# A recurrent attention block with a gated layer behind it: a triangular inverse in 33 instead of 37 schedule items, and a chunk's preparation one chunk later

## Chip, core and metric

The kernel runs on one core of a Trainium2 chip. A core has five engines with a queue of instructions each: the tensor engine (PE in the profile; PEld is its loading of weights), the vector engine (DVE), the scalar engine (ACT), GpSimd (POOL) and the sync engine (SP), which here issues nearly all DMA transfers. The metric is the device time of the whole kernel in microseconds, the median of several runs.

## What is computed

The first block is a recurrence over 768 time steps for 4 batches of 8 heads of width 40; its output is the input of a gated layer with 3072 tokens, width 320 and 2048 hidden units:

```python
for t in range(S):
    kt, vt, rt = (k[:, :, t], v[:, :, t], r[:, :, t])
    wt, at, bt = (w[:, :, t], a[:, :, t], b[:, :, t])
    y[:, :, t] = np.einsum('bhd,bhde->bhe', rt, state)
    Sa = np.einsum('bhde,bhe->bhd', state, at)
    state_decay = state * wt[:, :, None, :] - np.einsum('bhd,bhe->bhde', Sa, bt)
    state = state_decay + np.einsum('bhd,bhe->bhde', vt, kt)
...
h = x @ w_in
g = h * np.cos(h)
out = g @ w_out
```

## The kernel before, in words

Time is cut into 24 chunks of 32 steps. Within a chunk the recurrence is solved in closed form, for which a 32 by 32 lower triangular system per batch and head has to be inverted; from chunk to chunk only the state is handed on. The program issues every instruction in an order that is written out by hand: a list of segments for each chunk c (`segs`, lines 1056 to 1093), each segment a small function. The engines run their own queues in that order, so the list decides what stands ahead of what on each engine.

The segments are these.

- **Main work of chunk c** (`main`, line 954), which must follow the previous chunk: `t` (transposes of the state, tile sT), `q` (tile qps), `x` (tile x0ps, copied out by ACT at line 625 and DVE at line 626), `s` (tile sps: the inverse, `G["rt", c]`, times that copy, line 629), `z` (tile dps: the new state, DVE lines 682 and 689, POOL lines 683 and 694). Two steps after z the output y is written to DRAM and read back transposed as xT (`tokens`, line 699).
- **Preparation of the next chunk** (`p2`, line 946): `v`, `k`, `g` with tiles vT, kT, gram; g ends with DVE lines 567 and 573, which free the PSUM tile gram. All these PSUM tiles come from one pool of two buffers, `at` (line 325), so each one waits for the release of the last but one.
- **Preparation of two chunks at a time, well ahead** (`p1`, line 917): `pw` (W: eight transposes wT, ACT copies, POOL lines 381 and 392, and the reciprocal of W at line 396 with the product bn on POOL at line 397), `pa` (a~: eight transposes aps, DVE line 402 twice, and the reciprocal of the pair's second chunk), `pb` (b~: transposes bT) and `pn` (N: the matrices to invert, tile nps). pa also puts the loads of the next pair's w, a and b on SP, two and more steps later (lines 931 to 935).
- **The inverse of a group of four chunks** (`inverse`, line 507), all on DVE but for a POOL memset: a start (transpose, line 478), 31 steps with j from 31 down to 1 (a product, line 488, and a subtraction, line 492, over j(32 - j) elements per partition), an end (transpose, line 501). `s` of the group's first chunk can't be issued before the end has been.
- **Pieces of the gated layer**, each M in a list standing for one: A (`first_a`, tile ph, with three DVE sums of an earlier piece at lines 810 to 812), B (`first_b`, the rest of ph, then ACT line 759, DVE line 761, ACT lines 765 and 766, DVE line 769, where `turns` is h minus its rounding), and two S pieces (`second`/`products`, tile po). A of chunk pair g needs xT of that pair.

The function `step` (line 347) issues one segment or piece, then what has become due of the delayed work (`later`: loads, stores, copies), and then takes items of the pending inverse: one item a step from chunk 5 on. So an inverse is spread over some forty steps, one item behind each. Items may be empty; four of the 37 are, right behind the start. When a list comes to `s` and the inverse has not ended, lines 1105 to 1109 first issue one more piece with up to four items behind it.

The inverse of chunks 8 to 11 begins behind pn in chunk 6 and ends in chunk 8, that of 12 to 15 begins in chunk 10, and so on for 16 and 20. In the lists of before, W and a~ of chunks 12 and 13 are prepared in chunk 7 (those of 16 and 17 in 11, of 20 and 21 in 15), b~ and N of the same chunks in chunk 8 (12, 16); W and a~ of chunks 14 and 15 in chunk 9, b~ and N in chunk 10, behind which the next inverse begins. `scanned` (line 939) multiplies up the decays of a later group on DVE (lines 171 and 176, 4.0 us together) in chunks 4, 8 and 12.

Of the kernel before, what the change touches and what calls it, by code (L numbers as in the profile page):

```python
# [20 lines left out]
def kernel(  # L21
# [45 lines left out]
    P, C, DP = 128, 32, 64  # L67
# [53 lines left out]
    for n, fill in (("w", 1.0), ("a", 0.0), ("b", 0.0)):  # L121
        for i in range(4):
            x = slice((i - 2) * H * DP, (i - 1) * H * DP)
            if i < 2:
                t = const.tile([P, H, DP], F32, tag=f"nat_{n}{i}", name=f"nat_{n}{i}")
            else:
                t = {
                    "w": w_in_sb[:, 0, late:], "a": w_in_sb[:, 1, late:], "b": late_out
                }[n][:, x].rearrange("p (h d) -> p h d", h=H)
# [4 lines left out]
    for n in "kvr":  # L134
        t = const.tile([P, H, D], F32, tag=f"nat_{n}", name=f"nat_{n}")
# [370 lines left out]

    def inverse(c):
        return [
            lambda: inv_start(c), *[lambda: None] * (4 if c >= 8 else 0),
            *(lambda j=j: inv_step(j) for j in range(C - 1, 0, -1)), lambda: inv_end(c)  # L510
        ]


# [448 lines left out]
    with tc.manual_schedule():  # L962

        w_work = weights()
        w_count = [0]

        def counted(work):
            work()
            w_count[0] += 1

        w_steps.extend([w_work[0][1], w_work[1][1], w_work[0][2]])
        for n, (*_, product) in enumerate(w_work):
            nxt = n + 5 if n < 5 else n + 3 if n >= 7 else len(w_work)
            w_steps.append(lambda f=product: counted(f))
            if nxt < len(w_work):
                w_steps.append(w_work[nxt][0])
            if n + 1 < len(w_work):
                w_steps.append(w_work[n + 1][2])
            if n + 2 < len(w_work):
                w_steps.append(w_work[n + 2][1])  # L980

        def all_of(steps, n=None):
            for work in steps[:n]:
                work()
            del steps[:n]

        def busy(n, after=False):


            ps = ps_h.tile([P, 512], F32, tag="h", name="busy")  # L990
            if after:
                nc.vector.memset(tick, 1.0)
                nc.tensor.matmul(
                    ps[:1, :], lhsT=tick, rhs=pick(idle, 0, (0, 4), (1, P)), start=True, stop=True, skip_group_check=True
                )
            for _ in range(n):
                mm(ps, idle, pick(idle, 0, (0, 4), (1, P)), True)

        def shifted(n):


            ps = at("pad")
            for _ in range(n):
                mm(ps[:1, 0, :1], idle[:, :1], idle[:, :1], True)


        G["w1"] = sb2.tile([P, 2, 4 * B, C], F32, tag="gT", name="w1")
        nc.vector.memset(G["w1"], 0.0)
        first, other = p1(0), p1(2)
        for seg in (*first[:2], *other[:2], *first[2:], *other[2:]):  # L1010
            step(seg)
        scanned(1)
        p2_in(0)
        p2_kn(0)
        inv_steps.extend(inverse(0))
        v, k, g = p2(0)
        v1, k1, g1 = p2(1)
        for n, seg in ((12, v), (0, k), (0, g), (6, main(0)[2]), (6, None), (4, v1), (0, k1), (0, g1)):
            for _ in range(n):
                inv_steps.pop(0)()  # L1020
            if seg:
                step(seg)
            else:
                for m in range(3):
                    w_work[m][0]()
                p2_in(1)
                p2_kn(1)
        N_PAD = {0: 111, 19: 75}
        shifted(N_PAD[0])
        while inv_steps:  # L1030
            inv_steps.pop(0)()
            if 2 < len(inv_steps) < 9:
                busy(1, True)
        for m in range(3, 5):
            w_work[m][0]()

        done = 0

        def piece(*fill):
            nonlocal done  # L1040
            _, work, j, need = pieces[done]
            while w_steps and w_count[0] < need[j]:
                w_steps.pop(0)()
            step(work, *fill)
            done += 1

        def allowed(c):
            return done < len(pieces) and 2 * pieces[done][0] + 2 <= c

        M = object()  # L1050
        for c in range(NCH):
            t, q, x, s, z = main(c)
            v, k, g = p2(c + 1) if c + 1 < NCH else [lambda: None] * 3
            q0 = c - c % 4 + 4
            fill, pn, pn4 = (1, 4), None, None
            if c == 0:
                segs = [s, z]
            elif c == 1:
                segs = [t, v, q, k, x, g, s, z]
            elif c == 2:  # L1060
                segs, fill = [t, v, q, k, M, x, M, g, M, s, M, z, M, M], (0, 2)
            elif c == 3:
                pw4, pa4, pb4, pn4 = p1(4)
                pw, pa, pb, pn = p1(6)
                segs = [
                    t, pw4, M, q, pa4, M, x, lambda: scanned(2), M, s, pw, M, pb4, pa, M, pn4, M, z, M,
                    pb, v, pn, k, M, g,
                ]
                fill = (2, 3)
            elif c == 4:  # L1070
                pw, pa, *p8 = p1(8)
                segs = [t, v, M, q, M, k, x, M, M, M, M, pw, s, M, z, M, g, M, pa, lambda: scanned(3)]
                fill = (2, 0)
            elif c == 5:
                pw, pa = p1(10)[:2]
                pb, pn = p8
                segs = [t, M, pb, q, M, pn, k, M, x, M, s, pw, v, M, z, M, g, M, pa, M]
            elif c % 4 == 0 and q0 < NCH:
                pb, pn = p1(q0)[2:]
                segs = [t, v, M, q, M, k, x, M, g, M, s, pb, M, z, M, pn, M, M]  # L1080
                if q0 + 4 < NCH:
                    segs.insert(-1, lambda: scanned(c // 4 + 2))
            elif c % 4 == 1 and q0 < NCH:
                pw, pa = p1(q0 + 2)[:2]
                segs = [t, M, pw, q, M, x, k, M, s, v, M, z, M, pa, M, g, M, M]
            elif c % 4 == 2 and q0 < NCH:
                pb, pn = p1(q0 + 2)[2:]
                segs = [t, M, pb, q, M, pn, v, M, x, M, s, k, M, g, M, z, M, M]
            elif c % 4 == 3 and q0 + 4 < NCH:
                pw, pa = p1(q0 + 4)[:2]  # L1090
                segs = [t, M, pw, q, M, x, k, M, s, v, M, z, M, pa, M, g, M, M]
            else:
                segs = [t, v, M, q, M, x, k, M, g, M, s, M, M, z, M, M]
            n = len(segs)

            goal = 8 * (c + 1) - (18 if c < 19 else 20)
            empty, places = 0, segs.count(M)
            if c > 3:
                empty = max(0, min(places - (goal - done), 2 if c < 8 else places))
                goal = max(goal, done + places - empty)  # L1100
            place = 0
            if c == 19:
                shifted(N_PAD[c])
            for i, seg in enumerate(segs):
                while seg is s and ("rt", c) not in G:
                    if allowed(c):
                        piece(4, 0)
                    else:
                        inv_steps.pop(0)()
                while seg is pn4 and w_steps:  # L1110
                    w_steps.pop(0)()
                if seg is not M:
                    step(seg, *fill, small=seg in (q, x, g, s, z, pn, pn4))
                    if c < 2 or c == 2 and not done:
                        busy({s: 6, q: 5, v: 4, k: 4, z: 4}.get(seg, 3))
                else:
                    place += 1
                    if place * empty // places > (place - 1) * empty // places:
                        continue
                    if allowed(c) and (c != 4 or done < 23):  # L1120
                        piece(*fill)
                while i == n - 1 and c > 3 and done < goal and c != 4 and allowed(c):
                    piece(*fill)
                if seg is pn and (c == 3 or c > 4 and c % 4 == 2):
                    inv_steps.extend(inverse(q0))
        for g, work, j, _ in pieces[done:]:
            if g == NCH // 2 - 1 and j == 0:
                while waiting:
                    step(lambda: None)
            step(work)  # L1130
        while waiting:
            step(lambda: None)
# [29 lines left out]
```

## Time and profile before

| | before |
|---|---|
| time, median of 3 runs (lowest to highest) | 854.71 us (853.95 to 854.74) |
| span of the profiled execution | 849.2 us |
| PE busy in it | 738.0 us (87%) |
| DVE busy | 582.4 us (69%) |
| ACT busy | 378.7 us (45%) |
| POOL busy | 248.6 us (29%) |
| mean clock granted to PE | 0.937 |
| one reciprocal, DVE line 396 | 2.14 us |
| start and end of an inverse, DVE lines 478 and 501 | 1.24 and 1.93 us |

The page of the profile gives each engine's busy time, and below it the span in 40 equal slices, each digit the busy share in tenths. A line of a wait list reads "engine, tile and line that waited <- engine, tile and line that released it: us in total, times, longest". A line of a timeline begins with the start in us from the beginning of the span and the duration in us; "out<-in" are the program's names for the tiles, followed by shapes and, in brackets, the idle time of the engine just before and what ended it.

### The profile page before, as it was taken

How to read it: one execution, taken by the hardware profiler on the slowest of the kernel's cores; microseconds unless marked ns; L12 is line 12 of the kernel's file. 1: busy time of each engine (PE TensorE's matmuls, PEld its weight loads, DVE VectorE, ACT ScalarE, POOL GpSimd, SP SyncE). 2: the span in 40 equal slices, each digit the busy share in tenths (PEclk: the TensorE clock that was granted, in tenths of full speed). 3: DMA queues.
4: the chain of work that ended last, by engine and by line, in shares of the span. 5: the costliest groups of instructions: out<-in, count | busy, mean ns of one | idle time of the engine just before them, and what ended most of it. 6: DMA issues, size and time to landing. Idle time of an engine off the chain costs nothing.

```text
span 849.2 us, 38915 instructions
## 1 busy us (share of the span) xinstructions
PE 738.0 (87%) x17312; PEld 614.7 (72%) x17312; DVE 582.4 (69%) x1266; ACT 378.7 (45%) x697; POOL 248.6 (29%) x420
## 2 busy tenths in 40 slices
PE   3557778896899988999978999889999897999996
PEld 2434456674577877888867888768888787888875
DVE  6988878778734788675897664997466865444444
ACT  1216686454254425345435444534653442453442
POOL 5305544220524531231430331331233132122100
PEclk9758789998989989999998999999999998999999
DMA  7367562353243314234223323223220220201000
GB/s 122 82 128 217 132 159 77 55 123 55 55 100 66 69 24 76 52 95 70 54 40 61 71 55 67 50 47 59 46 44 25 39 43 21 40 20 35 20 16 15
DMA packets 183302, 55.74 MB, mean 66 GB/s; under 512 B 157152, under 2 KB 178656, under 8 KB 183136
## 3 DMA queue, kind: packets, MB, share of 16 engines
q1 hardware_dynamic: 180560, 51.95, 28.8%
q8 instruction: 136, 2.23, 1.1%
q10 hardware_dynamic: 2320, 0.98, 0.6%
q0 software_dynamic: 256, 0.33, 0.2%
q14 instruction: 30, 0.25, 0.1%
HBM read 42.07 MB, written 11.14 MB: 63 GB/s over the span
## 4 chain that ended last, share of the span: by engine, by line
PE 55%; DVE 20%; ACT 8%; DMA 5%; SPq 5%; issue 5%; POOL 3%; POOLq 0%; DVEq 0%; ACTq 0%
PE ph L102 21%; PE po L102 14%; SPq L153 5%; PE dps L102 4%; DVE inv_tmp L488 3%; PE x0ps L102 2%; PE vT L331 2%; DVE rw L396 2%; DVE turns L761 2%; ACT turns L766 2%; PE sps L102 2%; PE gram L102 2%; PE nps L102 2%; ACT turns L765 2%; DVE inv L492 1%
## 5 line engine op out<-in xcount | busy, mean ns | idle before, releaser
L102 PE MATMUL ph<-xT,w_in_sb 128*128 128x256 f32 x768 | 193.5, 398 | 5.4 <-DVE gT L769 4.6
L102 PEld LDWEIGHTS ph<-xT,w_in_sb 128*128 128x128 f32 x768 | 144.2, 197 | 35.5 <-issue 14.6
L759 ACT ACTIVATE turns<-ph,rnd 128x512 f32<-128x512 f32 x96 | 64.0, 686 | 173.9 <-PE ph L102 173.5
L761 DVE SCALAR_TENSOR_TENSOR turns<-turns,ph 128x512 f32<-128x512 f32 x96 | 63.4, 679 | 75.8 <-ACT turns L759 75.2
L102 PE MATMUL po<-w_out_sb,gT 128*128 128x160 f32 (+1 forms) x448 | 100.0, 353 | 0.4 <-DVE gT L769 0.4
L683 POOL TENSOR_TENSOR qz<-qz,wc 128x160 f32<-128x160 f32 x92 | 44.2, 499 | 158.4 <-DVE qz L682 157.8
L769 DVE TENSOR_TENSOR gT<-ph,turns 128x512 f32<-128x512 f32 x96 | 65.7, 686 | 34.1 <-ACT turns L766 34.1
L102 PEld LDWEIGHTS po<-w_out_sb,gT 128*128 128x128 f32 x448 | 71.8, 194 | 13.8 <-issue 3.6
L765 ACT ACTIVATE turns<-turns 128x512 f32<-128x512 f32 x96 | 60.2, 627 | 39.1 <-DVE turns L761 39.1
L102 PE MATMUL po<-t,gT 128*128 128x160 f32 x320 | 71.3, 305 | 0.0
L766 ACT ACTIVATE turns<-turns,half_pi 128x512 f32<-128x512 f32 x96 | 69.3, 722 | 3.1
L102 PE MATMUL po<-w_out_sb,s 128*128 128x160 f32 x304 | 58.7, 309 | 0.6 <-DVE ot L849 0.6
L102 PE MATMUL ph<-xT,w_in_tail 64*128 64x256 f32 x384 | 54.8, 403 | 0.0
L102 PEld LDWEIGHTS po<-t,gT 128*128 128x128 f32 x320 | 53.7, 195 | 0.0
L102 PEld LDWEIGHTS po<-w_out_sb,s 128*128 128x128 f32 x304 | 47.3, 194 | 2.4 <-issue 1.2
L841 POOL TENSOR_TENSOR s<-gT,s 128x256 f32<-128x256 f32 x36 | 28.6, 794 | 55.8 <-DVE s L811 55.8
L682 DVE TENSOR_TENSOR qz<-dps,qz 128x160 f32<-128x160 f32 x92 | 28.9, 315 | 23.3 <-PE dps L102 23.1
L396 DVE RECIPROCAL rw<-nat_w 128x320 f32<-128x320 f32 x20 | 42.8, 2141 | 0.0
L102 PEld LDWEIGHTS ph<-xT,w_in_tail 64*128 64x128 f32 x384 | 33.4, 187 | 9.9 <-issue 6.2
L492 DVE TENSOR_TENSOR home<-home,inv_tmp 128x31 f32<-128x31 f32 (+15 forms) x93 | 37.9, 407 | 3.2
L572 ACT COPY vvm<-gram 128x256 f32<-128x256 f32 x24 | 8.8, 368 | 67.8 <-DVE ag L567 67.8
L397 POOL TENSOR_TENSOR bn<-nat_b,rw 128x320 f32<-128x320 f32 x22 | 19.6, 889 | 60.8 <-DVE rw L396 52.4
(157 smaller groups left out, 1433.1 us busy)
## 6 DMA issues: line engine op xcount, KB each, us to landing
words<-in_moe_w_in_dram SPq DMA_DIRECT2D x8, 512.0 KB
nat_k<-in_k_dram SPq DMA_DIRECT2D x96, 40.0 KB
nat_v<-in_v_dram SPq DMA_DIRECT2D x96, 40.0 KB
nat_r<-in_r_dram SPq DMA_DIRECT2D x96, 40.0 KB
xd<-yt SPq DMA_DIRECT2D x48, 80.0 KB
out_dram<-ot SPq DMA_DIRECT2D x24, 160.0 KB
nat_b<-in_b_dram SPq DMA_DIRECT2D x88, 40.0 KB
wd<-ws SPq DMA_DIRECT2D x5, 640.0 KB
```

The costliest lines, as they stand in the source:

```text
L102: nc.tensor.matmul(o, lhsT=lhsT, rhs=rhs, start=start, stop=stop, skip_group_check=True)
L153: via.dma_start(nat[n, c][blk[i], :, :D], at_c.rearrange("h t d -> t h d"))
L396: nc.vector.reciprocal(rw, wn)
L492: nc.vector.tensor_tensor(x[:, j:, :j], x[:, j:, :j], tmp, ALU.subtract)
L682: nc.vector.tensor_tensor(z, pick(dp, 0, (2 * N72 + C, 2), (N72, 2), (1, D)), z, ALU.add)
L683: nc.gpsimd.tensor_tensor(z, z, wc.rearrange("p (f m b) -> p f m b", f=2, m=2)[:, :, :, bb] .unsqueeze(3).to_broadcast([P, 2, 2, D]), ALU. ...
L759: nc.scalar.activation(n, u, ACTF.Identity, bias=rnd, scale=1.0)
L761: nc.vector.scalar_tensor_tensor(n, n, -ROUND, u, ALU.add, ALU.subtract)
L765: nc.scalar.activation(n, n, ACTF.Abs)
L766: nc.scalar.activation(n, n, ACTF.Sin, bias=half_pi, scale=-2.0 * math.pi)
L769: nc.vector.tensor_tensor(gT[:, 2 * e : 2 * e + 2].rearrange("p f t -> p (f t)"), us[e], ns[e], ALU.mult)
L841: (nc.vector if g == NCH // 2 - 1 else nc.gpsimd).tensor_tensor(s4[:, 2 * j : 2 * j + 2], gT[:, 1::2, toks_of(0)], s2, ALU.subtract)
```

## The change

The inverse gets one empty item instead of four from chunk 8 on, and its last two steps (j of 2 and 1, 60 and 31 elements per partition) share an item; with that it has 33 items in place of 37, and both its beginning and its end move forward in the order. The preparation of W and a~ for chunks 12 and 13 (16 and 17, 20 and 21) leaves the chunk in which an inverse is under way and goes into the next one, behind `s`, by which time the inverse has ended. The b~ and N of the same chunks go one chunk further too, into the chunk that also prepares W and a~ of the next pair. What is computed stays the same; the number of M places in each list stays 8.

```diff
     def inverse(c):
         return [
-            lambda: inv_start(c), *[lambda: None] * (4 if c >= 8 else 0),
-            *(lambda j=j: inv_step(j) for j in range(C - 1, 0, -1)), lambda: inv_end(c)
+            lambda: inv_start(c), *[lambda: None] * (c >= 8),
+            *(lambda j=j: inv_step(j) for j in range(C - 1, 2, -1)), lambda: [inv_step(j) for j in (2, 1)],
+            lambda: inv_end(c)
         ]
...
             elif c % 4 == 0 and q0 < NCH:
-                pb, pn = p1(q0)[2:]
-                segs = [t, v, M, q, M, k, x, M, g, M, s, pb, M, z, M, pn, M, M]
+                pw, pa = p1(q0)[:2]
+                segs = [t, v, M, q, M, k, x, M, g, M, s, pw, M, z, M, pa, M, M]
                 if q0 + 4 < NCH:
                     segs.insert(-1, lambda: scanned(c // 4 + 2))
             elif c % 4 == 1 and q0 < NCH:
+                pb, pn = p1(q0)[2:]
                 pw, pa = p1(q0 + 2)[:2]
-                segs = [t, M, pw, q, M, x, k, M, s, v, M, z, M, pa, M, g, M, M]
+                segs = [t, M, pb, q, M, x, k, M, pn, M, s, pw, v, M, z, M, pa, M, g, M]
             elif c % 4 == 2 and q0 < NCH:
                 pb, pn = p1(q0 + 2)[2:]
                 segs = [t, M, pb, q, M, pn, v, M, x, M, s, k, M, g, M, z, M, M]
             elif c % 4 == 3 and q0 + 4 < NCH:
-                pw, pa = p1(q0 + 4)[:2]
-                segs = [t, M, pw, q, M, x, k, M, s, v, M, z, M, pa, M, g, M, M]
+                segs = [t, M, q, M, x, k, M, s, v, M, z, M, M, g, M, M]
```

## Prediction before the change was run

> **What bounds the kernel now.** I read the page first, then the tensor engine's waits by stretch, then both engines' timelines in the stretches where it waits. The first view is the page's busy time and its slices:
>
> ```profile
> PE 738.0 (87%) x17312; PEld 614.7 (72%) x17312; DVE 582.4 (69%) x1266; ACT 378.7 (45%) x697; POOL 248.6 (29%) x420
> ...
> PE   3557778896899988999978999889999897999996
> ...
> DVE  6988878778734788675897664997466865444444
> ```
>
> The tensor engine (PE) is the bound, but once a group of four chunks it dips just where the vector engine (DVE) reaches 8 or 9 tenths. These are the inverses. The next view is busy time by stretch, one row for each inverse of a group from chunk 8 on (start of the group's first transpose to use of its result; columns: stretch, busy PE, PEld, DVE, ACT, POOL, granted clock, DMA):
>
> ```profile
> 273.00:341.00 68.00, 61.42 (x1523) 52.36 (x1516) 56.62 (x125) 28.22 (x53) 23.07 (x40) 0.92 0.31 57
> 395.00:464.00 69.00, 61.69 (x1577) 53.45 (x1576) 57.55 (x131) 28.68 (x55) 19.72 (x33) 0.95 0.31 56
> 518.00:585.00 67.00, 59.07 (x1533) 51.23 (x1514) 56.98 (x131) 27.99 (x53) 18.86 (x31) 1.00 0.30 55
> 639.00:706.00 67.00, 58.38 (x1566) 50.81 (x1551) 49.79 (x127) 26.89 (x51) 17.05 (x27) 0.97 0.16 34
> ```
>
> PE idles 6.6, 7.3, 7.9 and 8.6 us in them. Between them (341 to 400, 464 to 518, 585 to 650) its waits sum to 0.8, 0.2 and 1.2 us, so the gain is to be had in these four stretches or not at all. PE's list of waits in 395 to 470 (who waits for whom: us in total, times, longest) names the cause:
>
> ```profile
> PE vT L331 <- DVE vvm L573: 3.9, 1, 3.9
> PE sps L102 <- DVE x L626: 2.4, 1, 2.4
> ```
>
> The same list for 640 to 712 has something else on top, the last transpose of the inverse itself:
>
> ```profile
> PE sps L102 <- DVE home L501: 4.4, 1, 4.4
> ```
>
> The DVE timeline of chunk 11 shows the queue ahead of the copy L626, for which s of chunk 11 waits:
>
> ```profile
> 419.11 2.15 DVE L396 RECIPROCAL rw<-nat_w 128x320 f32<-128x320 f32 x1
> 421.17 0.33 DVE L488 TENSOR_TENSOR inv_tmp<-home,rt 128x220 f32<-128x220 f32 x1
> 421.53 0.93 DVE L492 TENSOR_TENSOR rt<-rt,inv_tmp 128x220 f32<-128x220 f32 x1
> ...
> 423.66 1.27 DVE L761 SCALAR_TENSOR_TENSOR turns<-turns,ph 128x512 f32<-128x512 f32 x2
> ...
> 426.07 0.46 DVE L626 COPY x<-x0ps 128x288 f32<-128x288 f32 x1 [0.38 <-ACT x L625]
> ```
>
> No idle time from 410.0 to 425.7: DVE sets the pace here, and the reciprocal of W's preparation stands in that queue.
>
> [...] after the 3.9 us wait four vT transposes took 1.09 us (0.60 to 0.66 elsewhere), after the 4.4 us wait pairs of po started every 0.53 us for 0.27; of four waits of 2.3 to 2.4 us one was followed by it (at 671, where PE stopped for its own issue). [...] L492 at 220 elements took 0.93 us beside bn (POOL L397, 0.87), and 0.39 elsewhere.
>
> **The change, part by part.** From undisturbed rows one inverse step (L488 and L492) lasts 0.40 + 0.0020 n us, n = j(32 - j): 0.91 at n = 256, 0.71 at 156.
>
> *Items, 37 to 33.* Three of four empty items go, so from x of chunk 10 (6, 14, 18) on, each step of the schedule carries the inverse step that three items later carried before. The last two steps share an item, so the end comes four items earlier. No DVE work disappears: three steps move ahead of z of chunk 10, where DVE idles 1.7, 0.9, 0.4 and 1.2 us at a time (402 to 409). The added wait is that of the first step for the POOL memset, which ends 1.3 us after the transpose (397.2 to 398.5). Behind it in DVE's queue stand a step, the output sums L849 and sm of chunk 10, for which PE comes at 399.3. Counted at nothing.
>
> *W and a~ out of chunks 7, 11, 15.* Each loses two reciprocals (2.06 us from start to next start), two L402 (1.20), about 0.95 and 0.65 us that bn costs neighbours, and on PE eight wT and eight aps transposes (0.97 and 0.9). Walk through 395 to 464:
>  - First wait. From qz (410.0) to the start of turns (423.66) stand steps 27 to 21 now, 24 to 19 then: 5.43 against 5.07 us. So turns starts 2.06 + 0.36 + 0.95 = 3.4 us earlier, at 420.3; I take 420.7, since a longer step 25 comes ahead of qz. The chain on to s takes 2.9 us as before: s at 423.6. PE without wT is there at 426.59 - 2.39 - 0.97 = 423.2. The wait falls from 2.4 to about 0.4.
>  - Second wait. s to vT takes 20.9 us; it loses step work (10 steps, n = 2455, against 9, n = 2163: 0.98), L402 1.20, reciprocal 2.06 and bn 0.65: 4.9, leaving 16.0. PE alone needs 447.47 - 3.88 - 426.59 - 0.9 = 16.1. The wait is gone or below 1: vT at 440.2 +- 0.6 for 447.47, so 7.0 us taken.
>  - The half rate after it: eight vT and eight ph took 5.3 us for some 2.75: 2.6 back.
>  - The moved transposes run in chunk 12 instead: 1.9 to pay, since PE is full there.
>  Sum 7.7. For 273 to 341 the same walk gives vT at 316.7 for 325.69 (9.0, the first half-rate stretch in it), 1.7 for the second half-rate stretch, less 1.9: 8.8. For 518 to 585: 7.0 (part of the 7.8 is held back by a 1.7 us issue stall), plus 1.2 for waits at 584 and 586, less 1.9: 6.3.
>
> *Chunk 20.* No preparation there. Now the end of the inverse is reached only in an extra piece put ahead of s (line 1107), which first forces the two L769. By the new order it is queued after k, around 693, and needs 1.9 us; PE reaches s at about 699.7 without that piece. The 4.4 us wait and the 3.0 us of half rate behind it go: 7.4.
>
> *The moved work in chunks 8, 9 (12, 13; 16, 17).* At s of chunk 8 DVE has gaps of 2.0 and 1.3 us, and z, whose sums come next in its queue, ends 4.4 us of PE work after s (wT 1.0, A 1.8, z 1.6): room for a reciprocal. a~ behind B: L402, reciprocal and two L769 take 4.9 us, product 0 after 4.3; PE comes back to that ph after S, S and t, 4.2 us: 0.1 us. The scan (4.0 us) queues behind, ahead of the sums, which S needs 6.8 us after A: nothing. In chunk 9 b~ and N stand apart by a piece or more, with ACT at 45%: nothing. pw ahead of z puts 2.1 us before A's sums: PE needs 3.8 us to z. Nothing.
>  Loads for chunks 14 and 15 now leave in chunks 8 and 9: 24 issues at 0.49 us, 12 us, among k, v, r of chunk 11. From the issue rows I estimate that b of 14 lands some 24 us after aps: the queue is free after 4, k, v, r take 6.3, w and a of both chunks 8.8, the scan's store and b 2.8, landing 2. The reciprocal of 14 ends after some 20.5 (18 us of PE work from aps to s of chunk 9, then 2.1 and the copies). bn may thus wait up to 4 us on POOL (the trace has one such wait of 4.4), holding the state's product behind it about 1 us. xd of chunk 9 then leaves A of chunk 10 less slack: 9.4 us from z to A for 11.2. From 0 to 2 us a group; I take 1, 3 in all.
>
> *Chunks 0 to 7.* inverse(0) loses one filling matmul block, inverse(4) still ends in the same extra piece with its 7.5 us wait: nothing, +- 1.
>
> Sum: 8.8 + 7.7 + 6.3 + 7.4 - 3.0 = 27.2; 854.7 - 27.2 = 827.5, say 828.
>
> **The rivals.** (1) *Waits shrink, the clock does not recover.* [...] half rate costs 1.7 to 3.4 us in each of four groups, the steps brought forward meet POOL more often (1 us each way). 4 x 2.3 + 4 x 1 = 13 us less: 840. For it: halving followed one 2.4 us stall. Against: none in 518 to 585. (2) *Only chunk 20 gains*: DVE still sets the pace in the windows, or the waits reappear one chunk later: 847. Against: PE waits nothing there now and DVE has several us of gaps. (3) *Slower*: nothing gained in the three windows, bn's wait of 4.4 us on the loads stops the state chain in each group (13.2), only 7.4 won: 860. For it: late loads already held POOL's vp copy 7.7 us at 339.7, with no wait of PE. (4) *More*: the 3 us of new waits and the 1 to 1.5 us that I leave in each window vanish too: about 820.
>
> **How the numbers follow.** Main case 0.56, around 828; (1) 0.20; (2) 0.07; within 0.2% 0.03; (3) 0.08; (4) 0.06. The range 819 to 848 takes in the main case, (1), (2) and most of (4), 0.85 less the tails of the main case. Faster 0.89, same 0.03, slower 0.08.
>
> **What would show it.** PE's waits of 2 to 4 us for L626 and L573 in chunks 7, 11, 15 gone or under 1 us; no L396 inside the inverse's stretch; no wait of s in chunk 20 for L501; granted clock 1.0 in these stretches. Wrong: PE waiting for ph (DVE L769), for xT or for bT (POOL bn) in chunks 8 to 10, or halved clock after waits under 2 us.

## The result, and the profile after

| | before | after |
|---|---|---|
| time, median (lowest to highest) | 854.73 us (853.95 to 855.52) | 832.42 us (829.26 to 834.83) |
| after over before, 95% interval | | 0.9746 (0.9708 to 0.9784) |
| span of the profiled execution | 849.2 us | 831.2 us |
| mean clock granted to PE | 0.937 | 0.949 |

Four runs stand behind each median. The change saves 22.3 us (18.5 to 25.0) in the median. The traces show less: the profiled execution of before took 850.9 us, 3.8 less than its median, and the two profiled spans differ by 18.0 us. The kernel after, run again beside other experiments, took 830.11 us against 849.66 of before there, a ratio of 0.9766 (0.9733 to 0.9799). From line 511 on the lines of the kernel after stand one higher: L626 is now L627, L573 is L574, L769 is L770; L396 and the lines of the inverse keep theirs.

First the page of after, its busy times and slices (a digit is the busy share of a fortieth of the span in tenths; PEclk the granted clock):

```profile
PE 729.9 (88%) x17310; PEld 606.1 (73%) x17310; DVE 585.2 (70%) x1265; ACT 379.0 (46%) x697; POOL 248.3 (30%) x420
...
PE   3547778897879989999999999999999999999996
...
DVE  6988787869644799855898755898457975444544
...
PEclk9758799999789999999999999999999999999999
```

The PEclk row of the page of before, for comparison:

```profile
PEclk9758789998989989999998999999999998999999
```

DVE does the same work (585.2 us for 582.4), but the slices in which it reaches 8 or 9 no longer pull PE down: from slice 16 on PE stays at 9 to the last but one. The clock's 8s of before from slice 15 on are gone.

Here is one row for each inverse of after from chunk 8 on, from the start of its first transpose (L478) to the start of its last (L501); the rows in the prediction ran on to the use of the result (columns: stretch, busy PE, PEld, DVE, ACT, POOL, granted clock, DMA):

```profile
274.00:328.00 54.00, 50.75 (x1377) 42.85 (x1359) 48.42 (x117) 24.44 (x46) 21.43 (x35) 1.00 0.29 55
392.00:446.00 54.00, 51.97 (x1353) 45.02 (x1348) 48.23 (x123) 24.11 (x46) 17.49 (x27) 1.00 0.29 55
510.00:565.00 55.00, 52.86 (x1357) 45.61 (x1350) 48.93 (x123) 24.35 (x47) 17.47 (x27) 1.00 0.29 56
627.00:679.00 52.00, 50.57 (x1428) 44.27 (x1411) 43.94 (x117) 23.05 (x45) 15.11 (x24) 1.00 0.17 38
```

Between these two transposes an inverse takes 52 to 55 us instead of 65 to 66, PE idles 3.3, 2.0, 2.1 and 1.4 us in the rows, and the clock is full in all four.

PE's waits of after from 150 to 832 us (who waits for whom: us in total, times, longest):

```profile
PE sps L102 <- DVE rt L501: 7.5, 1, 7.5
PE nps L102 <- ACT bT L434: 4.2, 2, 3.9
...
PE sps L102 <- DVE x L627: 2.9, 3, 2.0
...
PE vT L331 <- DVE vvm L574: 2.5, 4, 0.7
PE ph L102 <- DVE gT L770: 2.1, 6, 0.4
PE ph L102 <- DMA xT<-xd: 1.8, 3, 0.9
```

Nearly all of the first two lie before 270, where the change does nothing. s of chunk 20 waits for L501 no more (4.4 us before). The waits for x and vvm, 2.4 and 3.9 us in chunk 11, are 0.7 and 0.7 there now. Waits of ph for gT and for xT have grown, from 0.8 and 0.6 us in the same part of before; in the stretches that took on the moved work they are new. The DVE timeline of chunk 11 (start, duration, instruction) shows why x is early:

```profile
412.27 0.39 DVE L488 TENSOR_TENSOR inv_tmp<-home,rt 128x220 f32<-128x220 f32 x1
412.69 0.39 DVE L492 TENSOR_TENSOR rt<-rt,inv_tmp 128x220 f32<-128x220 f32 x1
...
417.29 1.28 DVE L762 SCALAR_TENSOR_TENSOR turns<-turns,ph 128x512 f32<-128x512 f32 x2
...
419.70 0.46 DVE L627 COPY x<-x0ps 128x288 f32<-128x288 f32 x1 [0.35 <-ACT x L626]
```

No reciprocal stands ahead of x, and L492 at 220 elements takes 0.39 us where it took 0.93 beside bn.

**Where the time went, by half group.** I cut both traces at the first matmul of z of chunks 6, 8, 10, 12, 14, 16, 18 and of the last chunk, 23. A stretch from z of chunk 6 to z of chunk 8 (z 6 to 8 for short) holds an inverse, one from z of 8 to z of 10 the work that was moved into it. Six of these rows of before (columns as above):

```profile
283.81:347.08 63.27, 56.44 (x1298) 49.45 (x1297) 53.59 (x119) 26.76 (x50) 18.64 (x31) 0.92 0.28 54
347.08:408.01 60.93, 60.36 (x1585) 52.56 (x1585) 37.02 (x82) 29.88 (x56) 16.99 (x30) 1.00 0.35 76
408.01:470.26 62.25, 54.75 (x1297) 47.55 (x1296) 52.77 (x119) 26.75 (x50) 17.04 (x28) 0.95 0.27 50
470.26:530.63 60.37, 60.28 (x1586) 52.41 (x1586) 36.99 (x82) 29.95 (x56) 17.20 (x30) 1.00 0.31 65
530.63:591.05 60.42, 52.29 (x1297) 45.91 (x1296) 52.66 (x119) 26.78 (x50) 17.10 (x28) 1.00 0.27 53
591.05:650.90 59.85, 59.85 (x1586) 52.29 (x1585) 33.60 (x73) 29.85 (x56) 16.80 (x30) 1.00 0.19 40
```

The same six of after:

```profile
284.97:339.19 54.22, 50.43 (x1282) 43.95 (x1282) 49.57 (x111) 25.80 (x48) 18.01 (x30) 1.00 0.22 46
339.19:404.16 64.97, 62.97 (x1601) 54.48 (x1600) 41.36 (x91) 31.08 (x58) 16.83 (x30) 1.00 0.42 83
404.16:457.22 53.06, 50.41 (x1281) 44.00 (x1280) 48.28 (x110) 25.80 (x48) 16.86 (x28) 1.00 0.21 44
457.22:522.90 65.68, 62.80 (x1602) 54.29 (x1601) 41.76 (x91) 31.11 (x58) 16.82 (x30) 1.00 0.37 72
522.90:575.12 52.22, 50.45 (x1281) 44.08 (x1280) 47.83 (x110) 25.80 (x48) 16.82 (x28) 1.00 0.21 45
575.12:639.34 64.22, 62.62 (x1601) 54.22 (x1600) 37.74 (x84) 31.09 (x58) 17.24 (x31) 1.00 0.27 53
```

Each inverse stretch gives up 16 matmuls (the moved transposes), each following one takes on 16. Idle is length less PE's busy time:

| stretch | length, change | PE busy, change | PE idle, before and after |
|---|---|---|---|
| z 6 to 8 | -9.05 | -6.01 | 6.83, 3.79 |
| z 8 to 10 | +4.04 | +2.61 | 0.57, 2.00 |
| z 10 to 12 | -9.19 | -4.34 | 7.50, 2.65 |
| z 12 to 14 | +5.31 | +2.52 | 0.09, 2.88 |
| z 14 to 16 | -8.20 | -1.84 | 8.13, 1.77 |
| z 16 to 18 | +4.37 | +2.77 | 0.00, 1.60 |
| z 18 to 23 | -6.52 | -2.84 | 9.36, 5.68 |

The sum is -19.2 us; 1.2 us are lost ahead of z of 6, which leaves the 18.0 of the spans. From z 14 to 16, where no half rate occurred before, the busy time falls by the 16 transposes alone, 1.84 us. Taking the same 1.84 for the other two, the half rate was 6.01 - 1.84 = 4.2 us of the first row's gain and 4.34 - 1.84 = 2.5 us of the third row's. The rest is idle time.

### The profile page after: what moved, and what is told of

Same layout as the page of the kernel before. It is cut to its first block, busy times and chain, and to the rows that moved or that the text cites. A ratio compares the mean times of both kernels' runs of the same rounds, so it can differ in the third digit from the quotient of the medians.

```text
span 831.2 us, 38876 instructions
## 1 busy us (share of the span) xinstructions
PE 729.9 (88%) x17310; PEld 606.1 (73%) x17310; DVE 585.2 (70%) x1265; ACT 379.0 (46%) x697; POOL 248.3 (30%) x420
## 4 chain that ended last, share of the span: by engine, by line
PE 49%; DVE 22%; ACT 8%; DMA 7%; SPq 6%; issue 5%; POOL 3%; POOLq 0%; DVEq 0%; ACTq 0%
PE ph L102 19%; PE po L102 12%; SPq L153 5%; DVE inv_tmp L488 4%; PE dps L102 3%; PE x0ps L102 3%; DVE turns L762 2%; PE gram L102 2%; DVE gT L770 2%; PE sps L102 2%; ACT turns L767 2%; DVE inv L492 2%; DVE rw L396 2%; PE vT L331 1%; PE nps L102 1%
## 5 line engine op out<-in xcount | busy, mean ns | idle before, releaser
L102 PE MATMUL ph<-xT,w_in_sb 128*128 128x256 f32 x768 | 189.2, 392 | 8.9 <-DVE gT L770 5.9
L102 PEld LDWEIGHTS ph<-xT,w_in_sb 128*128 128x128 f32 x768 | 141.6, 193 | 40.3 <-issue 15.3
L770 DVE TENSOR_TENSOR gT<-ph,turns 128x512 f32<-128x512 f32 x96 | 64.7, 680 | 27.3 <-ACT turns L767 27.3
L102 PE MATMUL po<-t,gT 128*128 128x160 f32 x320 | 69.6, 299 | 0.0
L573 ACT COPY vvm<-gram 128x256 f32<-128x256 f32 x24 | 8.9, 370 | 78.4 <-DVE ag L568 78.4
L396 DVE RECIPROCAL rw<-nat_w 128x320 f32<-128x320 f32 x20 | 42.9, 2143 | 1.2 <-POOL kn L524 1.1
L102 PEld LDWEIGHTS ph<-xT,w_in_tail 64*128 64x128 f32 x384 | 33.9, 189 | 10.2 <-issue 6.2
L492 DVE TENSOR_TENSOR home<-home,inv_tmp 128x31 f32<-128x31 f32 (+15 forms) x93 | 35.9, 386 | 3.2
L381 POOL COPY wc<-wb 128x16 f32<-128x16 f32 x24 | 5.0, 209 | 108.8 <-ACT wb L379 101.9
```

The lines of the kernel that those rows point to most:

```text
L102: nc.tensor.matmul(o, lhsT=lhsT, rhs=rhs, start=start, stop=stop, skip_group_check=True)
L396: nc.vector.reciprocal(rw, wn)
L492: nc.vector.tensor_tensor(x[:, j:, :j], x[:, j:, :j], tmp, ALU.subtract)
L770: nc.vector.tensor_tensor(gT[:, 2 * e : 2 * e + 2].rearrange("p f t -> p (f t)"), us[e], ns[e], ALU.mult)
```

## The experiments

The theory is that DVE's queue sets the pace in chunks 7, 11 and 15 (reciprocals, L402 and inverse steps stand ahead of what PE waits for), and that in chunk 20 the end of the inverse does. Its rivals: only one of the two parts works; the clock, not the queue, is what matters; something else in the moved work is.

### One part alone

The first of two kernels has only the items of the change:

```diff
-            lambda: inv_start(c), *[lambda: None] * (4 if c >= 8 else 0),
-            *(lambda j=j: inv_step(j) for j in range(C - 1, 0, -1)), lambda: inv_end(c)
+            lambda: inv_start(c), *[lambda: None] * (c >= 8),
+            *(lambda j=j: inv_step(j) for j in range(C - 1, 2, -1)), lambda: [inv_step(j) for j in (2, 1)],
+            lambda: inv_end(c)
```

> The kernel before with the inverse in 33 items alone; W, a~, b~ and N stay where they were. My theory: only chunk 20 gains (4.4 us of wait and 3.0 us of half rate) and the 1.2 us of waits for the inverse's end in chunk 16; the waits for L626 and L573 in chunks 7, 11 and 15 stay at 2 to 4 us, the first some 0.6 us longer, since larger steps meet the reciprocal: 846 to 850 us. Rival, that the earlier beginning of the inverse is what takes the load off DVE: the waits of chunks 7, 11 and 15 fall as well, below 840 us.

Measured: 848.22 us, ratio 0.9960 (0.9944 to 0.9976). The wait of s in chunk 20 is gone, and that group gains 6.2 us. The other three change by -0.5, -0.8 and +1.7 us, since the waits of chunks 7, 11 and 15 stay. PE's waits of this kernel from 270 to 712:

```profile
PE sps L102 <- DVE x L627: 10.3, 3, 4.2
PE vT L331 <- DVE vvm L574: 8.5, 3, 2.9
```

The waits for x even rose, in chunk 7 from 3.35 to 4.15 us and in chunks 11 and 15 from 2.4 to 3.1, about the 0.6 that was expected of larger inverse steps ahead of x; the reciprocal is still there.

The second has only the moved lists:

```diff
-                pb, pn = p1(q0)[2:]
-                segs = [t, v, M, q, M, k, x, M, g, M, s, pb, M, z, M, pn, M, M]
+                pw, pa = p1(q0)[:2]
+                segs = [t, v, M, q, M, k, x, M, g, M, s, pw, M, z, M, pa, M, M]
...
+                pb, pn = p1(q0)[2:]
                 pw, pa = p1(q0 + 2)[:2]
-                segs = [t, M, pw, q, M, x, k, M, s, v, M, z, M, pa, M, g, M, M]
+                segs = [t, M, pb, q, M, x, k, M, pn, M, s, pw, v, M, z, M, pa, M, g, M]
...
-                pw, pa = p1(q0 + 4)[:2]
-                segs = [t, M, pw, q, M, x, k, M, s, v, M, z, M, pa, M, g, M, M]
+                segs = [t, M, q, M, x, k, M, s, v, M, z, M, M, g, M, M]
```

> The kernel before with the preparation moved alone; the inverse keeps its 37 items. My theory: the waits for L626 and L573 in chunks 7, 11 and 15 shrink to under 2 us, but the lists are two steps shorter by then, so the inverse's end is only queued behind g of chunks 8, 12 and 16 and s waits for it some 1.6 us; chunk 20 keeps its wait of 4.4 us: 844 to 849 us. Rival, that the move is the whole of the change and the items do nothing: 832 to 836 us.

Measured: 853.15 us, ratio 1.0022 (1.0002 to 1.0041), where 844 to 849 was expected: a miss. The waits for x and vvm fell as the theory has it, but another took their place. PE's waits of this kernel from 270 to 712:

```profile
PE sps L102 <- DVE ot L849: 10.5, 3, 3.5
PE sps L102 <- DVE home L501: 4.4, 1, 4.4
PE vT L331 <- DVE vvm L573: 2.6, 3, 0.9
```

s of chunks 8, 12 and 16 now waits 3.5 us each. The list names L849, the last instruction to end before; the DVE timeline shows what s needs:

```profile
333.35 0.42 DVE L573 TENSOR_TENSOR vvm<-gram,su 128x256 f32<-128x256 f32 x1 [0.44 <-ACT vvm L572]
333.69 1.90 DVE L501 STREAM_TRANSPOSE home<-home 128x1024 f32<-128x1024 f32 x1
335.44 1.60 DVE L849 TENSOR_TENSOR ot<-ot,po 128x160 f32<-128x160 f32 x5
```

L501 ends at 335.59, s starts at 335.74. The inverse's end is queued behind g, one step ahead of s, and PE comes there earlier now. The granted clock then was 0.51 for 6.8 us from 334.6, and for 3.4 us behind the same wait of chunk 12. I had expected waits of 1.6 us and none of this half rate.

So the parts do not add: alone they are worth -3.3 and +1.7 us on the medians, together about -20. In this kernel taking work out of the inverse's stretch is worth nothing unless the inverse also ends items earlier, and ending it earlier is worth little while the reciprocals stand in it.

### The disputed instruction: the reciprocal

In before, six reciprocals inside the inverse's stretches become copies of the same shape. This leaves out the division for chunks 12, 13, 16, 17, 20 and 21.

```diff
-        nc.vector.reciprocal(rw, wn)
+        if c >= 12 and c % 4 < 2:
+            nc.vector.tensor_copy(rw, wn)
+        else:
+            nc.vector.reciprocal(rw, wn)
```

> The kernel before, in its own order, with the six reciprocals of chunks 12, 13, 16, 17, 20 and 21 replaced by copies of W: the division is left out there, so what is timed is DVE without some 1.8 us at each of those six places. If DVE's queue sets the pace in the three stretches, the first waits fall from 3.4, 2.4 and 2.4 to 1.6, 0.6 and 0.6 us, the second from 3.2, 3.9 and 2.3 to 1.4, 2.1 and 0.5, and most of the half rate behind them goes: 838 to 844 us. If PE waits for something else there (loads, POOL, the order of PSUM buffers), the waits stay: 853 to 855 us.

Measured: 838.9 us, ratio 0.9865 (0.9829 to 0.9900). The copy in DVE's timeline of chunk 11:

```profile
413.95 0.32 DVE L397 COPY rw<-nat_w 128x320 f32<-128x320 f32 x1
```

It takes 0.32 us for 2.14. In this kernel L626 has become L629, and L573 L576. PE's waits of this kernel in the stretch of chunk 7 (273 to 341):

```profile
PE sps L102 <- DVE x L629: 1.6, 1, 1.6
PE vT L331 <- DVE vvm L576: 1.4, 1, 1.4
```

In chunks 11 and 15 they are 0.6 and 2.1, and 0.6 and 0.5. Each of the six waits is shorter by 1.7 to 1.8 us, just what was taken out of DVE's queue ahead of it. The three groups gain 4.6, 4.5 and 3.3 us; chunk 20's wait of 4.4 us stays, and its group gains 0.7. Nothing but six DVE instructions was changed, in what they compute and how long they take, so DVE's queue did set PE's pace there. The reciprocal takes 1.8 us more than the copy here, 6.7 times its time.

### Does the wait or the half clock behind it cost?

If PE is kept busy with useless matmuls during the wait of vT, the wait is still spent; if idle time is what brings the half rate, the clock then stays up. The first form has ten zero matmuls behind ACT's copies of t in chunks 8 and 12:

```diff
             nc.scalar.copy(G["s"][:, 4 * i : 4 * i + 4].rearrange("p i e -> p (i e)"), ps[:, i])
+        if c in (8, 12):
+            for _ in range(10):
+                mm(ps[:, 0], idle, pick(idle, 0, (0, 4), (1, P)), True)
```

> The kernel before with ten matmuls of zeros (128x512, bf16) behind t of chunks 8 and 12, in the two waits for L573 of 3.2 and 3.9 us; no wait is taken away, PE is only kept busy in it. If the waits bring the half rate, vT and ph behind them run at full rate: 4.3 us less, 849 to 852 us, and the stretches from 326.7 and 446.1 with clock 0.5 are gone. If the half rate comes from something else: 854 to 856 us.

Measured: 861.63 us, ratio 1.0136 (1.0097 to 1.0175). The wait wasn't filled, so this does not answer the question: the filler overwrites what ACT reads and so waited 4.9 us for ACT (L588), then ran at half rate (ten in 4.43 us; eleven take 2.54 in the second form) and held vT up until 330.7 us, 5 us later than in before. In the second form eleven stand ahead of t's transposes:

```diff
         G["s"] = sb1.tile([P, 2 * B, P], F32, tag="s", name="s")
+        if c in (8, 12):
+            for _ in range(11):
+                mm(ps[:, 0], idle, pick(idle, 0, (0, 4), (1, P)), True)
```

> The kernel before with eleven matmuls of zeros (128x512, bf16, some 2.3 us) ahead of the transposes of t in chunks 8 and 12, into the PSUM tile that these overwrite; the first try had them wait for ACT's copy of that tile. vT behind them waits for DVE in any case, until 325.7 and 447.5; its wait falls from 3.2 and 3.9 us to about 1 and 1.6, and no work of the kernel is taken away. If the idle time is what brings the half rate, vT and ph run at full rate behind it: 3 to 4 us less than the kernel before, a ratio of 0.995 to 0.997. If it comes from something else: a ratio of 1.000 to 1.002.

Measured: 851.48 us, ratio 0.9985 (0.9962 to 1.0007). As a time this lies between the two forecasts and decides nothing, and the trace is of an execution of 859.5 us, 8 above the median; but it shows the two filled places. The PE timeline of this kernel at t of chunk 8:

```profile
322.05 2.54 PE L102 MATMUL sT<-idle 128*128 128x512 bf16 x11
...
326.27 0.63 PE L331 MATMUL vT<-ident,vp 128*128 128x128 f32 x4 [0.80 <-DVE vvm L573]
...
327.17 1.89 PE L102 MATMUL ph<-xT,w_in_sb 128*128 128x256 f32 x8
```

The same place in before:

```profile
325.69 0.63 PE L331 MATMUL vT<-ident,vp 128*128 128x128 f32 x4 [3.17 <-DVE vvm L573]
...
326.62 3.56 PE L102 MATMUL ph<-xT,w_in_sb 128*128 128x256 f32 x8
```

vT starts no earlier, as DVE sets it, but the eight ph behind it take 1.89 us instead of 3.56, and in chunk 12 they take 1.89 instead of 3.62. In both places the half rate went with the idle time, though the wait's end stayed: it is a cost apart from the wait. Elsewhere in this execution it came back: for 6.8 us behind a stall of 2.4 us at 374.7 for which the trace shows no releaser (an issue stall), and for 3.4 us behind the wait for x in chunk 11, 2.4 us in both kernels, which cost none in before. That fits the small gain of the total, but no run shows it for the median.

### What keeps the gain from being larger

The kernel after was run again, as the measure for the next three:

> The changed kernel once more, as the measure for the other three on the same chip: a ratio of 0.97 to 0.98 to the kernel before.

Measured: 830.11 us, given above. In after, bn (L397) of chunk 14 waits 5.0 us for its load, and holds up the POOL products of z of chunk 9, and with them xT. Here is POOL's timeline of after in chunk 9:

```profile
371.82 0.86 POOL L397 TENSOR_TENSOR bn<-nat_b,rw 128x320 f32<-128x320 f32 x1 [4.99 <-DMA nat_b<-in_b_dram]
372.64 1.71 POOL L684 TENSOR_TENSOR qz<-qz,wc 128x160 f32<-128x160 f32 x4
374.31 1.28 POOL L695 TENSOR_TENSOR yt<-yt,wb 128x512 f32<-128x512 f32 x1
```

So the next kernel loads b ahead of a there:

```diff
-                        8 + m // 3 if c == 2 else (9 if c == 6 else 2) + m, lambda m=m: load(c + 2 + m % 2, "wab"[m // 2])
+                        8 + m // 3 if c == 2 else (9 if c == 6 else 2) + m, lambda m=m: load(c + 2 + m % 2, ("wba" if c >= 12 and c % 4 == 0 else "wab")[m // 2])
```

> The changed kernel with the loads for chunks 14, 15 (18, 19; 22, 23) issued in the order w, b, a instead of w, a, b. My theory is that bn of chunk 14 waits 5.0 us on POOL for b to land, holds the state's product and y behind it, and so brings the waits for xT ahead of A in chunks 10 and 14: with b some 5 us earlier these waits (0.7, 1.0 and 0.3 us) go and the time falls by 1 to 3 us against the changed kernel. Rival: nobody who matters waits for that product; bn's wait goes and the time stays within 0.5 us, or a of 14 comes late for the transposes aps in chunk 9 and it gets slower by 1 to 3 us.

Measured: 837.73 us, ratio 0.9842 (0.9800 to 0.9884): no gain, but a loss of 7.6 us against after's 830.11. The trace does not show where: it is of an execution of 833.4 us, 4.3 below the median, and from z of 6 on that took as long as the repeat of after. bn waits 0.5 us, and PE's wait for xT is gone in these groups, which confirms that link. But PE's waits from 341 to 640 now begin thus:

```profile
PE aps L331 <- DMA nat_a<-in_a_dram: 1.8, 2, 0.9
```

With b ahead of a it is a that comes late: here the order of the loads only chose who waits.

The next wait in the list of after is that of nps for bT (L434), 3.9 us in chunk 5, where the change does nothing. This kernel gives that chunk the new order of its siblings:

```diff
-                segs = [t, M, pb, q, M, pn, k, M, x, M, s, pw, v, M, z, M, g, M, pa, M]
+                segs = [t, M, pb, q, M, x, k, M, pn, M, s, pw, v, M, z, M, pa, M, g, M]
```

> The changed kernel with chunk 5 in the order that the change gave to chunks 9, 13 and 17: N of chunks 8 and 9 a piece and two segments later, pa ahead of g. In both kernels PE waits 3.9 us there for the copies of bT (ACT, which is held by the scan on DVE) and runs at half rate from 234 on for 6.8 us. If N's place is what makes it wait, the 3.9 us and the 0.8 us behind it go, and most of 3.4 us of half rate: 4 to 8 us less than the changed kernel. If DVE behind the scan sets the pace there, the wait moves to x of chunk 5: within 1 us.

Measured: 832.12 us, ratio 0.9806 (0.9752 to 0.9859). That is no gain over after. The wait moved from N to x, with its whole length, as PE's waits from 200 to 270 show:

```profile
PE x0ps L102 <- ACT bT L434: 3.9, 1, 3.9
```

The next kernel has both edits at once, and pa one piece later in chunks 8, 12 and 16:

```diff
-                segs = [t, v, M, q, M, k, x, M, g, M, s, pw, M, z, M, pa, M, M]
+                segs = [t, v, M, q, M, k, x, M, g, M, s, pw, M, z, M, M, pa, M]
```

> The changed kernel with both of these, and with pa of chunks 8, 12 and 16 one piece later, so that A of the next chunk no longer finds its ph buffer held by the product behind pa's reciprocal (0.44 us in each of three groups). If the parts add up: 6 to 12 us less than the changed kernel, a ratio of 0.960 to 0.968 to the kernel before. If the waits only move: 0.970 to 0.975.

Measured: 836.74 us, ratio 0.9849 (0.9810 to 0.9887): slower than after by 6.6 us, where neither forecast had a loss of that size. In its trace the waits of ph for gT in chunks 8 to 17 are gone, but bT now waits for bn, three times and 4.3 us in all, and the 3.9 us stand at x. For the 3.9 us the remaining suspect was the scan of decays on DVE at the end of chunk 4, which went behind z of chunk 5:

```diff
-                segs = [t, v, M, q, M, k, x, M, M, M, M, pw, s, M, z, M, g, M, pa, lambda: scanned(3)]
+                segs = [t, v, M, q, M, k, x, M, M, M, M, pw, s, M, z, M, g, M, pa]
...
-                segs = [t, M, pb, q, M, pn, k, M, x, M, s, pw, v, M, z, M, g, M, pa, M]
+                segs = [t, M, pb, q, M, pn, k, M, x, M, s, pw, v, M, z, lambda: scanned(3), M, g, M, pa, M]
```

> The changed kernel with the scan for chunks 12 to 15 behind z of chunk 5 instead of at the end of chunk 4. It stands ahead of turns on DVE there; ACT waits for turns and so holds back its copies of bT, for which PE waited 3.9 us (moving N only moved that wait to x). If the scan is what holds the chain, the 3.9 us, the 0.9 us behind it and most of the half rate from 234 on go: 4 to 8 us less than the changed kernel, a ratio of 0.968 to 0.973. If the wait only moves into chunk 5's later part, or its store and the loads of chunk 12 come late: 0.975 to 0.980.

Measured: 835.71 us, ratio 0.9789 (0.9761 to 0.9818). Against before that is as good as after's 0.9766, no better. In the trace, of an execution of 840.8 us, the wait of nps is gone, so the scan's place did cause it; but now sT waits 3.6 us for vvm (L574), ahead of which the scan holds DVE from 251.0 to 257.0, and ph waits 1.9 us for xT where it waited 0.9. The wait moved with the scan.

### How many items the inverse needs

The last kernel is after with 35 items, two of them empty and the last two steps apart:

```diff
-            lambda: inv_start(c), *[lambda: None] * (c >= 8),
-            *(lambda j=j: inv_step(j) for j in range(C - 1, 2, -1)), lambda: [inv_step(j) for j in (2, 1)],
-            lambda: inv_end(c)
+            lambda: inv_start(c), *[lambda: None] * (2 if c >= 8 else 0),
+            *(lambda j=j: inv_step(j) for j in range(C - 1, 0, -1)), lambda: inv_end(c)
```

> The changed kernel's lists with an inverse of 35 items (two empty ones, the last two steps apart), halfway between 37 and 33. My theory: what counts is whether the inverse's end is queued ahead of g of chunks 8, 12 and 16, and in chunk 20 ahead of the extra piece; with 35 items it stands behind x of chunks 8, 12, 16 and behind g in chunk 20, so s waits for it nowhere over 1 us, and the time is that of the changed kernel within 3 us: a ratio of 0.976 to 0.981 to the kernel before. Rival: every item taken out brings its share of the difference between 37 and 33 items: a ratio of 0.986 to 0.992.

Measured: 834.5 us, ratio 0.9790 (0.9765 to 0.9815). PE's waits of this kernel from 330 to 700 begin:

```profile
PE sps L102 <- DVE home L501: 2.2, 3, 1.1
```

With one of chunk 16, named after the tile rt, s waits for the end of the inverse 1.1, 0.7, 0.9 and 0.5 us in chunks 8, 12, 16 and 20, where 37 items with the moved lists gave 3.5, 3.5, 3.5 and 4.4 and 33 give none. The time is the one forecast, and not the rival's 0.986 to 0.992: two of the four items get nearly all of the gain. The waits are short, and the granted clock is 1.00 from 274 to 711. The difference to 33 items lies within the intervals.

None of these kernels was faster than the change itself.

## Why the prediction was right, and where a term was off

The forecast of 828 us, in the case held likeliest, stands against 832.4 measured; the range held it. The mechanism came as forecast: the waits for x and vvm, the half rate behind them and the wait of chunk 20 went. The median flatters the sum. The 27.2 us were worked out on the trace of before, and between the two traces only 18.0 were gained. Of the 9.2 us that are missing, 5.0 are the cost of the moved work, 1.65 the stretch of chunk 7, 0.9 chunk 20, 0.4 the third row, and 1.2 were lost ahead of z of 6.

- **First wait, chunk 11.** Predicted to fall from 2.4 to about 0.4 us; it is 0.7. Up to z of 10 the kernel after is 3.85 us ahead, so s, at 420.2, corresponds to 424.1 in before's time, predicted 423.6. In chunk 7 more remains than the same walk had: 2.0 us, and the first row gained 9.05 for a predicted 8.8 + 1.9 = 10.7.
- **Second wait.** Below 1 us as predicted: 0.7, 0.7 and 0.6. vT of chunk 12 at 437.0 corresponds to 440.9; predicted 440.2 +- 0.6.
- **Half rate behind it.** Predicted 2.6 us back from z 10 to 12, measured 2.5; granted clock 1.00 from 274 to 711 in the trace of after. The third row as a whole gained 9.2 of 7.7 + 1.9 = 9.6, the fifth 8.2 of 6.3 + 1.9 = 8.2. The half-rate stretches of before and after (granted clock 0.5 in the traces) last 3.4, 6.8, 10.2 or 30.7 us, but for the one that the end cuts off: whole multiples of the shortest. What sets that length stays open.
- **Chunk 20.** There is no wait of s; the gain is 6.5 us for 7.4. A later issue stall of 1.25 us stands in front of a new stretch of half rate (3.4 us at 0.50 from 711.8), so not all of the 3.0 us counted back were kept.
- **Moved transposes, 1.9 us, and new waits, 1.0 a group: the mis-sized terms.** The stretches that took the work on grew by 4.0, 5.3 and 4.4 us instead of 2.9. Of this PE's busy time is 2.6, 2.5 and 2.8: by tile in the stretch from z of 12, aps and bT went from 1.0 to 2.1 us each, 2.2 together, the rest is spread. The growth of idle time is 1.4, 2.8 and 1.6. ph behind pa waits 0.44 us, predicted 0.1. bn waits 5.0 us on POOL for the load of b in the first two groups, predicted up to 4, and A of chunks 10, 14 and 18 then waits 0.7, 1.0 and 0.3 us (the second named after L568, and gone too with b loaded earlier), predicted about 1. Waits for L769 and for xT stood in the prediction as signs of being wrong; they came, but small. Not foreseen were issue stalls, which no releaser in the trace explains: from z of 12 to 14 one of 0.8 and one of 0.5 us where before had 0.1 of idle time in all.
- **Counted at nothing.** The memset behind the inverse's start, the scan behind B, b~ and N in chunk 9: none shows up as a wait of PE over 0.25 us. The chunks up to 6 lost 1.2 us, for the 1 that was allowed.
- **The rivals.** (1) fell, the clock did recover (1.00 from 274 to 711); that half rate would come back in each of four groups was an estimate of mine. (2), only chunk 20 gains, describes the kernel with 33 items alone: 848.2 for 847. (3) fell although its wait was longer than assumed: 5.0 us on POOL reached PE as 1 us or less. (4) fell by the mis-sized terms.

What the prediction didn't say is that neither part alone brings more than about a sixth of the gain. Its walk gave the chunk-20 gain to the items and the rest to the moved work; the second kernel shows that the items also carry chunks 8, 12 and 16, where s would have waited 3.5 us for an inverse of 37 items.

How PE's issue stalls come about, and where the busy time beyond the 2.2 us lies, stays open.

## What to carry to other kernels

When a long chain of small instructions is spread over a fixed number of schedule slots, look at two things together: what else stands in its engine's queue while it runs, and whether its last slot lies clear of the first use; easing only one can turn its gain into a wait at the other (here 3.5 us at s in the second kernel). Moving work out of a stretch where its engine sets the pace pays only if the stretch that takes it on has room on every engine that the work touches, loads included: here a group gained 8 to 9 us and gave 4 to 5 back. Count the half-clock time behind a wait as a cost of its own, since here it came to a quarter to a half of what the first two inverse stretches gained (2.5 of 9.2 us and 4.2 of 9.05).

## What the runs showed that I had not expected

- Some waits of 3.35 us and less were followed by half rate: in before the waits of 3.35 and 3.17 us of chunks 7 and 8, for 6.8 and 3.4 us, and in the repeat of the kernel after even a wait of 2.0 us at s of chunk 7, for 3.4 us. In the first profile of the same program a wait of the same length, 1.96 us, was not (granted clock 1.00), so two executions of one program can differ by it.
- PE stalls in issue by 0.4 to 2.4 us at places that move with the program order: 1.7 and 2.4 us in before, 0.5 to 1.3 in after, 2.4 in the filled kernel. They are about as large as the waits that are left.
- Two edits worth -0.4% and +0.2% alone were worth -2.5% together.
